# A seven-tap dynamic convolution followed by a maxout MLP: the first tokens' halo load is split into 112 and 15 partitions on two queues

## Chip, cores and metric

The kernel runs on one core of one Trainium2 chip. The metric is the device time of one execution in microseconds (us); three runs of the kernel before gave 476.36, 476.66 and 478.31, median 476.66. Profiles are of one further execution.

## What is computed

The reference takes x (8 x 4160 tokens x 192), a weight generator (8 heads x 7 taps per token) and three MLP matrices. Cut to its core:

```python
w = softmax(weight_gen, axis=-1)                      # per token and head, over K = 7 taps
x_pad = concatenate([zeros((B, 6, D)), x], axis=1)    # causal: 6 zero tokens ahead of each sequence
idx = arange(S)[:, None] + arange(7)[None, :]
a = einsum('bshk,bskhg->bshg', w, x_pad[:, idx, :])   # 8 heads of 24 channels
h1, h2 = a @ w1, a @ w2                               # 192 -> 1024
out = maximum(h1, h2) @ w_out                         # 1024 -> 192
```

A token's convolution needs the six tokens before it. Where tokens are cut into blocks, those six are the block's halo.

## The kernel before

**Tiling.** The 33,280 tokens are laid over 128 partitions, 260 consecutive tokens (CPP) each, so 16 partitions hold one sequence. They are worked in batches of 16 tokens per partition (BATCHES), and each batch in units of 8 (UNITS; 4 in batch 0). The halo of batch 0 on partition p is the last six tokens of partition p - 1: 6 x 192 floats, 4608 bytes, a row for each of partitions 1 to 127. Partition 0 has none and gets zeros (memset, L297), and each 16th partition begins a sequence, so its halo is multiplied by zero: a mask of 0 and 1 per partition (msk, L315 to L319) scales the halo on its way into xb_t (L324).

**Stages.** For a batch: ScalarE (ACT) takes exp of weight_gen (exp_sum, L109), VectorE (DVE) sums over taps (red, L114), ACT takes the log (ln, L117), DVE subtracts it (shift, L121), ACT's second exp gives normalized weights (weights, L134). DVE multiplies x by them for all seven taps (mul, L145) and adds the taps (adds, L162 to L164). The result must be transposed for TensorE (PE): in units 0 to 3 PE does it and sums the taps on the way (sum_transpose, L184, copied out by ACT, L190), later a DMA transpose (L171). The maxout is written as h1 + relu(h2 - h1): wd holds w2 - w1 (made by DVE at L375 to L380), hidden products are L209 and L220, relu is L231/L233 on ACT, and output products are L245, L254 and L259. The h1 part uses w10 = w1 @ w_out, which PE computes once from transposed w1 (L353, then L403).

**Order.** The program order on each engine is written out by hand (a manual schedule); each engine runs its instructions in that order, and waits for others by semaphores. DMAs are issued from two engines' queues: SyncE (SP) and GpSimd (POOL). Up to the loop the order that matters here is:

- SP: weight_gen of batch 0 (L87), the halo (L298), the first 4 tokens of x (xs, L303), w1 and w2 in pieces of 128 and 64 rows (ws0E, ws0T, ws1E, ws1T, L309), weight_gen of batch 1 (L87). No wait stands between them in the program.
- POOL: iota (L315), the identity matrix, then a copy (gate, L332) that reads ws0E, so that the loads behind it are issued only once ws0E has landed: x for the rest of batch 0 and for batch 1 (L97), w_out (L335), the batch halo by an SBUF copy (L103), weight_gen of batches 2 and 3. These x and w_out loads convert to bf16.
- ACT: exp_sum(0), the masked halo (L324), ln(0), the copy of xs (L327), weights(0), two copies of transposed w1 (L357), exp_sum(1), the copy of unit 0's transposed sum (L190).
- DVE: red(0), shift(0), mul(0,0), the five wd instructions, mul(0,4), red(1), mul(0,8); shift(1) after ln(1).
- PE: 50 dummy matmuls (keep_warm, L364), 24 transposes of w1 (L353), 12 dummies, sum_transpose(0), 16 dummies, then the hidden products of unit 0.

The halo's source and destination in the kernel before:

```python
nc.sync.dma_start(
    out=xs[1:P, 0:PAD * D],
    in_=bass.AP(tensor=x.tensor, offset=(CPP - PAD) * D,
                ap=[[CPP * D, P - 1], [1, PAD * D]]),
)
```

Of the kernel before, what the change touches and what calls it, by code (L numbers as in the profile page):

```python
# [23 lines left out]
def kernel(  # L24
# [9 lines left out]
    nc = tc.nc  # L34

    B, S, D = x.shape
    H, K = weight_gen.shape[2], weight_gen.shape[3]
    F = moe_w1.shape[1]
    P = 128
    PAD = K - 1  # L40
    WGC = H * K
    FCH = F // P
    CPP = B * S // P
# [246 lines left out]
    with tc.tile_pool(name="pstage", bufs=1) as pstage:  # L290
        ident_f = pstage.tile([P, P], FP32, name="ident_f")
        xs = pstage.tile([P, (PAD + 4) * D], FP32, name="xs")
        ws = {(kind, wi): pstage.tile([nr, F], FP32, name=f"ws{wi}{kind}")
              for kind, nr in (("E", P), ("T", 64)) for wi in range(2)}

        load_wg(0, nc.sync)
        nc.vector.memset(xs[0:1, 0:PAD * D], 0.0)  # L297
        nc.sync.dma_start(  # L298
            out=xs[1:P, 0:PAD * D],
            in_=bass.AP(tensor=x.tensor, offset=(CPP - PAD) * D,  # L300
                        ap=[[CPP * D, P - 1], [1, PAD * D]]),
        )
        nc.sync.dma_start(  # L303
            out=xs[:, PAD * D:],
            in_=bass.AP(tensor=x.tensor, offset=0, ap=[[CPP * D, P], [1, 4 * D]]),
        )
        for wi, wsrc in enumerate((moe_w1, moe_w2)):
            for kind, r0, nr in (("E", 0, P), ("T", P, 64)):
                nc.sync.dma_start(  # L309
                    out=ws[kind, wi],  # L310
                    in_=bass.AP(tensor=wsrc.tensor, offset=r0 * F, ap=[[F, nr], [1, F]]),
# [24 lines left out]
            out=wo[:, :].rearrange("p (f d) -> p f d", d=D),  # L336
            in_=bass.AP(tensor=moe_w_out.tensor, offset=0, ap=[[D, P], [P * D, FCH], [1, D]]),
# [198 lines left out]
```

## Time and profile before

| what | value |
|---|---|
| median of three runs | 476.66 us |
| the profiled execution | 477.96 us |
| its span, first to last instruction | 476.2 us |
| mean granted PE clock | 0.963 |
| PE busy | 435.2 us (91%) |
| DVE busy | 382.0 us (80%) |
| ACT busy | 356.6 us (75%) |
| POOL busy | 29.4 us (6%) |
| DMA bytes, mean rate | 65.84 MB, 138 GB/s |
| PE busy in the first 48 us | 20.07 us |

How to read it: the span is cut in 40 slices of 11.9 us, with one digit for each engine's busy share in tenths. PEclk is the clock that PE was granted, in tenths. The DMA row is the mean busy share of the core's 16 DMA engines, and GB/s what they moved. The chain that ended last is followed back from the last instruction, at each step to what released it; "SPq" in it is time in which SyncE's queue issues a DMA. The waits list which instruction waited for whom, in total. Landing times run from a DMA's issue to the end of its data. A busy PE is not a PE at its peak, since matmuls are pipelined and their ends are modelled.

### The profile page before, as it was taken

How to read it: one execution, taken by the hardware profiler on the slowest of the kernel's cores; microseconds unless marked ns; L12 is line 12 of the kernel's file. 1: busy time of each engine (PE TensorE's matmuls, PEld its weight loads, DVE VectorE, ACT ScalarE, POOL GpSimd, SP SyncE). 2: the span in 40 equal slices, each digit the busy share in tenths (PEclk: the TensorE clock that was granted, in tenths of full speed). 3: DMA queues.
4: the chain of work that ended last, by engine and by line, in shares of the span. 5: the costliest groups of instructions: out<-in, count | busy, mean ns of one | idle time of the engine just before them, and what ended most of it. 6: DMA issues, size and time to landing. Idle time of an engine off the chain costs nothing.

```text
span 476.2 us, 8966 instructions
## 1 busy us (share of the span) xinstructions
PE 435.2 (91%) x4014; PEld 290.9 (61%) x4014; DVE 382.0 (80%) x158; ACT 356.6 (75%) x405; POOL 29.4 (6%) x60
## 2 busy tenths in 40 slices
PE   4029998889989999999999999999999999999996
PEld 4017875456656666666666666666666666666675
DVE  2029499999999999999999999999999999990000
ACT  1033678977968888888888888889888878777762
POOL 0022101010101010101010101010100000000000
PEclk9556999999999999999999999999999999999999
DMA  1719357473778573848495847566684745333412
GB/s 56 210 37 177 81 147 141 157 162 100 188 138 207 125 206 103 213 92 204 89 209 109 198 133 161 169 143 186 123 179 111 181 105 137 100 94 92 94 73 100
DMA packets 60295, 65.84 MB, mean 138 GB/s; under 512 B 50369, under 2 KB 50881, under 8 KB 60256
## 3 DMA queue, kind: packets, MB, share of 16 engines
q1 hardware_dynamic: 53888, 41.03, 33.6%
q0 software_dynamic: 6368, 24.24, 23.2%
q8 instruction: 31, 0.51, 0.4%
q14 instruction: 8, 0.07, 0.0%
HBM read 35.96 MB, written 25.56 MB: 129 GB/s over the span
## 4 chain that ended last, share of the span: by engine, by line
PE 74%; ACT 14%; DMA 7%; SPq 3%; issue 1%; ACTq 0%
PE op_ps L259 29%; PE hdp L209 19%; PE hdp L220 13%; ACT rd_t L231 8%; PE op_ps L254 6%; DMA ws0T<-in_moe_w_dram 4%; ACT en_t L134 3%; DMA yt<-y_t 3%; PE yps L184 2%; SPq L303 2%; ACT o_t L271 2%; PE op_ps L245 2%; PE tp L353 1%; ACT rd_t L233 1%; PE warm L364 0%
## 5 line engine op out<-in xcount | busy, mean ns | idle before, releaser
L231 ACT ACTIVATE rd_t<-hdp 128x1024 bf16<-128x1024 f32 x240 | 246.5, 1029 | 63.8 <-PE hdp L209 36.7
L259 PE MATMUL op_ps<-wo,rd_t 128*128 128x192 bf16 x2080 | 214.3, 246 | 0.4 <-ACT rd_t L233 0.3
L145 DVE TENSOR_TENSOR m_t<-xb_t,en_t 128x21504 bf16<-128x21504 bf16 (+2 forms) x21 | 185.2, 8817 | 2.7 <-ACT en_t L134 2.5
L259 PEld LDWEIGHTS <-rd_t 128*128 128x128 bf16 x2080 | 175.7, 98 | 14.8 <-ACT rd_t L233 0.8
L209 PE MATMUL hdp<-yt,wdE 128*128 128x512 bf16 (+1 forms) x280 | 101.6, 364 | 4.8 <-DMA yt<-y_t 3.8
L209 PE MATMUL hdp<-yt,wdO 128*128 128x512 bf16 (+1 forms) x280 | 101.5, 364 | 0.0
L220 PE MATMUL hdp<-yt,wdR 64*128 64x512 bf16 (+1 forms) x560 | 84.6, 366 | 3.4 <-ACT rd_t L233 1.4
L162 DVE TENSOR_TENSOR m_t<-m_t 128x4608 bf16<-128x4608 bf16 (+1 forms) x31 | 78.0, 2515 | 0.5
L254 PE MATMUL op_ps<-w,yt 128*128 128x192 bf16 x260 | 65.3, 251 | 0.0
L220 PEld LDWEIGHTS <-wdR 64*128 64x128 bf16 x560 | 20.9, 94 | 66.7 <-issue 65.4
L254 PEld LDWEIGHTS <-yt 128*128 128x128 bf16 x260 | 25.1, 97 | 50.3 <-issue 36.0
L163 DVE TENSOR_TENSOR m_t<-m_t 128x3072 bf16<-128x3072 bf16 (+1 forms) x31 | 53.7, 1732 | 1.1
L271 ACT COPY o_t<-op_ps 128x768 f32<-128x768 f32 x65 | 51.9, 799 | 2.6 <-issue 2.6
L121 DVE TENSOR_TENSOR wg_t<-wg_t,sum_t 128x896 f32<-128x896 f32 (+1 forms) x17 | 17.7, 1043 | 31.1 <-ACT sum_t L117 31.1
L134 ACT ACTIVATE en_t<-wg_t 128x1024 bf16<-128x1024 f32 (+5 forms) x36 | 33.4, 937 | 0.4 <-DVE wg_t L121 0.4
L245 PE MATMUL op_ps<-w,yt 64*128 64x192 bf16 x260 | 32.5, 242 | 0.2 <-ACT w L409 0.2
L209 PEld LDWEIGHTS <-wdE 128*128 128x128 bf16 x280 | 27.4, 98 | 7.6 <-DMA yt<-y_t 4.3
L97 POOL DMA_DIRECT2D xb_t<-in_x_dram x20 | 10.9, 548 | 323.2 <-DVE m_t L145 323.2
L164 DVE TENSOR_TENSOR y_t<-m_t 128x1536 bf16<-128x1536 bf16 (+1 forms) x31 | 29.3, 945 | 1.1
L353 PE MATMUL tp<-ident_f,ws0E 128*128 128x128 f32 (+1 forms) x16 | 5.8, 390 | 25.0 <-DMA ws0E<-in_moe_w_dram 25.0
L209 PEld LDWEIGHTS <-wdO 128*128 128x128 bf16 x280 | 27.4, 98 | 1.9 <-issue 1.7
L233 ACT ACTIVATE rd_t<-hdp 128x1024 bf16<-128x1024 f32 x20 | 20.4, 1025 | 10.1 <-PE hdp L209 10.1
(40 smaller groups left out, 135.4 us busy)
## 6 DMA issues: line engine op xcount, KB each, us to landing
out_dram<-o_t SPq DMA_DIRECT2D x30, 768.0 KB, 3.7
xb_t<-in_x_dram POOLq DMA_DIRECT2D x14, 768.0 KB, 7.0
wg_t<-in_weight_gen_dram POOLq DMA_DIRECT2D x14, 448.0 KB, 7.8
xb_t<-xb_t POOLq DMA_DIRECT2D x16, 288.0 KB, 7.2
out_dram<-o_t SPq DMA_DIRECT2D x5, 384.0 KB, 2.3
wg_t<-in_weight_gen_dram SPq DMA_DIRECT2D x2, 448.0 KB, 9.9
xb_t<-in_x_dram POOLq DMA_DIRECT2D x4, 192.0 KB, 4.1
xb_t<-in_x_dram POOLq DMA_DIRECT2D x2, 384.0 KB, 7.2
```

The lines of the kernel that those rows point to most:

```text
L134: nc.scalar.activation(out=_sub(en_ts[b, o], k0 * N * 2, [[2 * N, k1 - k0], [2, N], [1, 2]]), in_=_sub(wg_ts[b], o * WGC + k0, [[1, k1 - k ...
L145: nc.vector.tensor_tensor(out=m_ts[b][:, K * o * D:K * (o + n) * D], in0=_sub(xb_ts[b], o * D, [[D, K], [1, n * D]]), in1=_sub(en_ts.pop(( ...
L162: nc.vector.tensor_tensor(out=taps(0, 1, 3), in0=taps(0, 1, 3), in1=taps(3, 1, 3), op=ALU.add)
L163: nc.vector.tensor_tensor(out=taps(0, 2, 2), in0=taps(0, 2, 2), in1=taps(1, 5, 2), op=ALU.add)
L164: nc.vector.tensor_tensor(out=y_ts[b][:, (o + a) * D:(o + a + w) * D], in0=taps(0, 1, 1), in1=taps(2, 1, 1), op=ALU.add)
L209: nc.tensor.matmul(hid_out(u, f, j), lhsT=wd[kind][:, f * P:(f + 1) * P], rhs=_sub(yt_ts[u], 2 * j * P, [[3 * P, n // 2], [1, P]]), start= ...
L220: nc.tensor.matmul(hid_out(u, f, j), lhsT=wd["R"][r, f * P:(f + 1) * P], rhs=_sub(yt_ts[u][r, :], P, [[3 * P, n // 2], [1, P]]), start=fir ...
L231: nc.scalar.activation(out=rd_ts[u][:, f, :], in_=hd_ts.pop((u, f)), func=AF.Relu)
L245: nc.tensor.matmul(op_ts[u, i // 2][:, at:at + D], lhsT=yt_ts[u][r, (3 * i + 1) * P:(3 * i + 2) * P], rhs=w10[r, 2 * D:3 * D], start=(i % ...
L254: nc.tensor.matmul(op[:, at:at + D], lhsT=yt[:, (3 * i + 2 * j) * P:(3 * i + 2 * j + 1) * P], rhs=w10[:, j * D:(j + 1) * D], start=False, ...
L259: nc.tensor.matmul(op[:, at:at + D], lhsT=rd[:, f, j * 512 + i * P:j * 512 + (i + 1) * P], rhs=wo[:, f * D:(f + 1) * D], start=False, stop ...
L271: nc.scalar.copy(out=_sub(o_ts[u], 4 * g * D, [[2 * D, 2], [D, 2], [1, D]]), in_=_sub(op_ts.pop((u, g)), 0, [[D, 2], [512, 2], [1, D]]))
```

## The change

The load of 127 halo rows from the SP queue becomes two: partitions 16 to 127 (112 rows) from the SP queue, in the same place, and partitions 1 to 15 (15 rows) from the POOL queue. Bytes, source, destination and all other instructions are the same. The new POOL DMA comes first in POOL's program, ahead of the iota and the identity. The reader of the halo, ACT's scaled copy, now waits for both. All later line numbers move up by one.

```diff
         nc.vector.memset(xs[0:1, 0:PAD * D], 0.0)
-        nc.sync.dma_start(
-            out=xs[1:P, 0:PAD * D],
-            in_=bass.AP(tensor=x.tensor, offset=(CPP - PAD) * D,
-                        ap=[[CPP * D, P - 1], [1, PAD * D]]),
-        )
+        for p0, p1, eng in ((16, P, nc.sync), (1, 16, nc.gpsimd)):
+            eng.dma_start(
+                out=xs[p0:p1, 0:PAD * D],
+                in_=bass.AP(tensor=x.tensor, offset=(p0 * CPP - PAD) * D,
+                            ap=[[CPP * D, p1 - p0], [1, PAD * D]]),
+            )
         nc.sync.dma_start(
             out=xs[:, PAD * D:],
             in_=bass.AP(tensor=x.tensor, offset=0, ap=[[CPP * D, P], [1, 4 * D]]),
```

## The prediction

> **What bounds the kernel now.** I read the page first: its slices, then the chain that ended last.
>
> ```profile
> span 476.2 us, 8966 instructions
> ...
> PE   4029998889989999999999999999999999999996
> ...
> PEclk9556999999999999999999999999999999999999
> DMA  1719357473778573848495847566684745333412
> ...
> PE 74%; ACT 14%; DMA 7%; SPq 3%; issue 1%; ACTq 0%
> ```
>
> One slice is 11.9 us. From the fourth slice on TensorE (PE) is busy nine tenths or more almost throughout, and the chain is mostly PE. The first three slices are different: PE is idle, its clock falls to half, and the chain's DMA and SPq shares sit there. So next the chain's own pieces, in order of time (start us, length us, what):
>
> ```profile
> 1.20 0.32 SPq L298
> ...
> 1.58 10.87 SPq L303
> ...
> 12.49 1.35 SPq L309
> ...
> 13.88 19.35 DMA ws0T<-in_moe_w_dram
> ...
> 33.27 6.12 PE tp L353 x23
> 39.39 1.40 PE warm L364 x12
> 40.79 4.25 PE yps L184 x42
> ```
>
> The end is set by an unbroken PE chain that begins at 33.27, when the second w1 piece (ws0T) has landed. Before it the SP queue stands in the issue of L303 for 10.87 us, right behind the halo (L298), and ws0T then takes 19.35 us for 256 KB. The waits say who feels it (total us, times, longest):
>
> ```profile
> POOL gate L332 <- DMA ws0E<-in_moe_w_dram: 31.2, 1, 31.2
> ...
> ACT xb_t L324 <- DMA xs<-in_x_dram: 25.5, 1, 25.5
> ...
> PE tp L353 <- DMA ws0E<-in_moe_w_dram: 25.0, 1, 25.0
> ```
>
> Last, stretches of the head. Columns after the length: busy us and (count) of PE, PEld, DVE, ACT and POOL, then granted clock, DMA share, GB/s.
>
> ```profile
> 8.00:12.00 4.00, 0.00 (x0) 0.00 (x0) 0.00 (x0) 0.00 (x0) 0.00 (x0) 0.82 0.06 26
> 12.00:20.00 8.00, 0.00 (x0) 0.00 (x0) 0.00 (x0) 0.00 (x0) 0.00 (x0) 0.50 0.75 213
> ...
> 28.00:32.00 4.00, 0.00 (x0) 0.00 (x0) 0.04 (x1) 1.52 (x3) 0.00 (x0) 0.50 0.06 26
> ```
>
> A share of 0.06 is 1/16: of 16 DMA engines one works, at 26 GB/s, both before and after the other loads pass (12 to 24 us).
>
> **What that engine carries.** The halo is 127 x 4608 B = 0.585 MB; a sixteenth of the SP loads after it (0.393 xs + 1.573 weights + 0.459 second weight_gen = 2.425 MB) is 0.152 MB. Together 0.737 MB, at 26 GB/s 28.3 us, from 3.7 us (first weight_gen in) to 32.0. The weight loads were complete at 32.6 to 33.2. So I read it thus: the whole halo goes through one engine, and each later load has a sixteenth queued there and is complete only after it. The other fifteen engines were done at 24.
>
> **Part 1: the 127-partition load becomes 112 (SP) + 15 (GpSimd).** [...]
>
> *New arrival times.* SP issues at 0.74 and then every 0.42 us (0.32 to 0.40 plus gaps in its rows): all eight by 4.1 us, ahead of the data; I assume no queue fills, since no engine has more than a sixteenth of anything. For the rate:
>
> ```profile
> DMA packets 728, 2.46 MB, mean 234 GB/s; under 512 B 88, under 2 KB 88, under 8 KB 728
> ```
>
> That is 13.0 to 23.5 us, these same loads on the fifteen free engines: 234 GB/s. The best in the trace is the first weight_gen load, 358 and 346 GB/s in its two full half-microseconds. I take 234, being the same loads. First weight_gen data end at 3.6 as now. Both halo parts and xs: 0.978 MB, 4.2 us, to 7.8. Add 0.5 (the first weight_gen data ended near 3.5, its Exp began at 4.04): ACT L324 starts at 8.3, now 30.48. ws0E and ws0T: 0.786 MB, 3.4 us, to 11.1, with the 0.5 **11.6**, now 33.27. PE's chain starts **21.7 us earlier**. At 350 GB/s it would start at 9.1 (24.2 saved), at 200 at 12.9 (20.4).
>
> *Does the rest follow?* What comes before PE's needs, now and shifted by 21.7: DVE needs 6.2 us from the start of L324 to the end of the first product (36.69 - 30.48): 14.5; PE wants it for L184 at 40.79 - 21.7 = 19.1. The wd matrices need ws1E and ws1T: 0.786 MB more, 15 us alone; then 3.8 us of DVE work (36.60 to 40.41), 18.8; PE wants them at 45.93 - 21.7 = 24.2. Both are covered by about 5 us. From 58 us to 125 DVE is without a gap and PE waits for it (yt, 5.0 and 8.2 us in the chain at 102 and 126), but DVE's last waits before that are for ACT results that follow PE, so DVE shifts with PE and gives nothing back.
>
> **Part 2: the new GpSimd DMA.** It stands in POOL's order before the iota and the identity. A POOL load row is 548 ns each (the w_out one 914): ident, now at 2.38, comes 0.55 to 0.9 late, PE's first 50 keep-warm matmuls (2.65 to 7.73) too; PE then idles till the weights come, so on the path 0. SP's x load and the weights are not behind it. ACT L324 now waits for it as well, and behind L324 in ACT's order stand the Ln, the copy of xs and the weights, so DVE. POOL loads of 192 KB, nearly three times its 68 KB, landed in 4.1 us (median), the slowest near them in 7.4: 15 rows issued at 0.84 are there by 5 to 9, and cover lasts until PE wants the first product: 19.1 - 6.2 = 12.9. Cost 0; each us later than 12.9 would cost one. Below nothing it can't go, beyond what part 1 counts.
>
> **Part 3: what the earlier gate triggers.** POOL's later loads wait on ws0E (gate, L332), now landing near 10.6 in place of 32.65. Today they have the engines to themselves:
>
> ```profile
> q0 software_dynamic: 1607, 1.36, 100.1%
> ```
>
> That row is 34.0 to 43.5 us: POOL's queue fills all 16 engines for 9.5 us. After the change, 1.1 MB of SP's loads (most of ws1E, ws1T, second weight_gen) are still under way when they start near 12. Alone those need 4.8 us; sharing half and half about 9.6, so the second weight_gen is in near 22, and POOL's loads end near 26. ACT's exp_sum(1) waits for the former and stands *before* the yt copy that PE needs; that copy is due at 45.08 - 21.7 = 23.4, so the Exp (0.95) must start by 22.4. Cover: 0.4 us, so between 0 (SP served first) and 4 us (POOL first: 26). I take **+0.7**. ws1T by 20, wd by 22, still under 24.2. POOL's own loads are wanted later: w_out at 30.4 (52.14 now), x for mul(1,0) at 36.6 (58.35 now), with L103 by 32: covered.
>
> **Part 4: the clock.** PE's matmuls ran 102 ns each in the first 50 and 106 in L184 at 40.8, but 60 in L184 at 49: the head works at half clock. The granted clock fell at 10.7, 3.0 us after the first block ended, stayed 0.50 through all 6 us of transposes and rose at 44.6, 5.3 us after dense matmuls began. [...] With the warm block ending near 8.3 the fall comes near 11.3, so at most the first transposes run fast. Between 0 and -4 (transposes and L184 at half their time, the rest then waiting for wd and exp_sum(1)); I take **-0.5**.
>
> **Sum.** -21.7 + 0.7 - 0.5 = -21.5 us. The profiled run took 477.96 (span 476.2 and 1.76 around it), so it would give 456.5. The runs' median is 476.66, 1.30 below the profiled one; from it: **455.2 us**, 4.5% faster.
>
> **The rivals.**
> - *Better than that* (0.11): loads near 350 GB/s, or the clock still up when the weights come: -24 to -28, 449 to 452.5. For: the first load's rate, and a shorter idle gap. Against: 234 for these very loads, and 0.50 through the transposes.
> - *The collision of part 3 bites* (0.12): the second weight_gen, or ws1T, lands 4 to 8 us later than PE wants it: 459 to 463. For: 0.4 us of cover. Against: 5 us of cover everywhere else.
> - *The split does not spread* (0.03): 112 partitions stay on one engine, 0.069 MB leaves it: 2.7 us, 474. Against: 64 partitions spread.
> - *Slower* (0.02): the GpSimd part lands late and holds ACT at L324, and with it DVE's whole head. By part 2 each us past 12.9 costs one, so the gain is gone when it lands at 34.4 and the kernel is 0.5% slower past 37; at 40, 479. Nearest rows say 4 to 7 us of flight, so it would have to take five times that.
>
> **How the numbers follow.** The likeliest case (0.72) is 452.5 to 459. Leaving out some of the first two rivals' ends, 450 to 461 holds about 8 in 10 and a little over. 0.5% (2.4 us) is about what can be told from no change here. Faster 0.95, within 0.03 (half of the third rival, and a chance of something unseen), slower 0.02.
>
> **What would show it.** Right: no stretch at a 0.06 share; SP's issues all under 1 us and done by 5; L324 near 8.3; tp near 11.6; yt copy at 23 to 24; L209 to the end as long as now (45.93 to 476). Wrong: SP still standing in an issue, tp after 13.5, ACT waiting at exp_sum(1) for more than 1 us, or a new DMA wait of DVE after 20 us. The prediction fails if the shift at the first tp does not arrive whole at the last matmul.

## The result and the profile after

| | before | after |
|---|---|---|
| median | 476.99 us (4 runs) | 454.19 us (4 runs) |
| profiled execution | 477.96 us | 453.83 us |
| its span | 476.2 us | 452.1 us |
| ACT's masked halo starts | 30.48 us | 7.06 us |
| first w1 transpose that needs ws0T | 33.27 us | 10.54 us |
| first hidden product (L209) | 45.93 us | 22.27 us |
| from there to the end of the span | 430.27 us | 429.83 us |

The ratio after to before is 0.9521 (95% interval 0.9495 to 0.9548): 4.8% faster. 455.2 was predicted, with a range of 450 to 461.

The page of the changed kernel, the rows that were shown of before:

```profile
span 452.1 us, 8967 instructions
...
PE   4999989899999999999999999999999999999996
...
PEclk9699999899999999999999999999999999999999
DMA  8936475637784839483957657393948363334312
...
PE 80%; ACT 15%; DMA 3%; issue 1%; SPq 0%; ACTq 0%
```

The hole in PE's second and third slice is gone, the DMA engines are busy from the first slice on, and the chain's DMA share has gone from 7% to 3%, its SPq share from 3% to 0%. The chain's head, in order of time (start, length, what):

```profile
1.20 0.41 SPq L299
1.67 0.42 SPq L304
2.12 0.43 SPq L310
2.60 7.90 DMA ws0T<-in_moe_w_dram
10.54 6.12 PE tp L354 x23
16.67 1.40 PE warm L365 x12
18.06 3.32 PE yps L184 x42
21.38 0.89 PE warm L365 x16
```

SP no longer stands in the issue of xs (0.42 us, 10.87 before), and ws0T takes 7.90 us in place of 19.35. The transposes last 6.12 us as before; PE's first sum takes 3.32 in place of 4.25, a matter of the clock (below). The waits of the first 60 us:

```profile
POOL gate L333 <- DMA ws0E<-in_moe_w_dram: 6.8, 1, 6.8
...
PE tp L354 <- DMA ws0E<-in_moe_w_dram: 2.1, 1, 2.1
ACT xb_t L325 <- DMA xs<-in_x_dram: 1.6, 1, 1.6
```

31.2, 25.0 and 25.5 us have become 6.8, 2.1 and 1.6. One stretch of the head in both kernels, 4 to 10 us, first after and then before (the last two columns are DMA share and GB/s):

```profile
4.00:10.00 6.00, 3.87 (x44) 3.51 (x41) 2.18 (x2) 3.46 (x5) 0.48 (x2) 0.98 1.03 291
```

```profile
4.00:10.00 6.00, 3.72 (x40) 3.55 (x37) 1.09 (x1) 0.95 (x1) 0.00 (x0) 1.00 0.06 25
```

All 16 engines at 291 GB/s where one moved 25. (The share of 1.03 is past 1, so records of packets overlap here; a share of about 1 is read as all sixteen busy.)

### The profile page after: what moved, and what is told of

Its sections match the earlier page's. It is cut to its first block, busy times and chain, and to the rows that moved or that the text cites. A ratio compares the mean times of both kernels' runs of the same rounds, so it can differ in the third digit from the quotient of the medians.

```text
span 452.1 us, 8967 instructions
## 1 busy us (share of the span) xinstructions
PE 435.1 (96%) x4014; PEld 290.5 (64%) x4014; DVE 382.3 (85%) x158; ACT 356.5 (79%) x405; POOL 29.7 (7%) x61
## 4 chain that ended last, share of the span: by engine, by line
PE 80%; ACT 15%; DMA 3%; issue 1%; SPq 0%; ACTq 0%
PE op_ps L259 32%; PE hdp L209 21%; PE hdp L220 14%; ACT rd_t L231 8%; PE op_ps L254 7%; ACT en_t L134 3%; ACT o_t L271 2%; PE yps L184 2%; PE op_ps L245 2%; DMA ws0T<-in_moe_w_dram 2%; PE tp L354 1%; DMA yt<-y_t 1%; ACT rd_t L233 1%; PE warm L365 1%; PE pw L404 0%
## 5 line engine op out<-in xcount | busy, mean ns | idle before, releaser
L209 PE MATMUL hdp<-yt,wdE 128*128 128x512 bf16 (+1 forms) x280 | 102.0, 365 | 2.9 <-DMA yt<-y_t 1.9
L209 PE MATMUL hdp<-yt,wdO 128*128 128x512 bf16 (+1 forms) x280 | 101.8, 365 | 0.0
L209 PEld LDWEIGHTS <-wdE 128*128 128x128 bf16 x280 | 27.5, 98 | 5.5 <-issue 3.0
L209 PEld LDWEIGHTS <-wdO 128*128 128x128 bf16 x280 | 27.5, 98 | 1.9 <-issue 1.7
L233 ACT ACTIVATE rd_t<-hdp 128x1024 bf16<-128x1024 f32 x20 | 20.4, 1024 | 10.2 <-PE hdp L209 10.1
L114 DVE TENSOR_REDUCE sum_t<-e_t 128x128 f32<-128x896 f32 (+1 forms) x17 | 17.7, 1041 | 9.2 <-ACT e_t L109 9.1
```

Source lines behind the costliest of these rows:

```text
L209: nc.tensor.matmul(hid_out(u, f, j), lhsT=wd[kind][:, f * P:(f + 1) * P], rhs=_sub(yt_ts[u], 2 * j * P, [[3 * P, n // 2], [1, P]]), start= ...
```

## Experiments

The theory: the halo's *number of partitions* decides over how many DMA engines SP's load is spread; with 127 it was one (0.06 of sixteen, 25 GB/s), and what stood behind it waited (ws0T took 19.35 us). The rivals: two queues, or a smaller transfer, make the gain. In all kernels here what is computed is unchanged. The last column is the span from the first hidden product on.

| kernel | ws0T's first transpose | first hidden product | span | rest |
|---|---|---|---|---|
| before | 33.27 | 45.93 | 476.2 | 430.27 |
| after | 10.54 | 22.27 | 452.1 | 429.83 |
| 113 + 14 | 30.76 | 42.09 | 472.0 | 429.91 |
| 112 + 15, both SP | 10.46 | 21.21 | 452.2 | 430.99 |
| 122 + 5 | 23.89 | 35.21 | 465.6 | 430.39 |
| 127 from GpSimd | 11.09 | 21.74 | 451.8 | 430.06 |
| 127 from ACT | 19.04 | 52.92 | 483.4 | 430.48 |
| 15 rows late | 10.88 | 26.41 | 456.5 | 430.09 |
| xs cut too | 10.68 | 22.86 | 453.7 | 430.84 |
| w1 first | 8.38 | 22.11 | 452.4 | 430.29 |
| after, again | 10.92 | 21.73 | 451.6 | 429.87 |
| w1 first, 36 dummies | 8.61 | 21.02 | 452.1 | 431.08 |
| 85 dummies first | 10.63 | 21.64 | 452.9 | 431.26 |

From the first hidden product on, every kernel takes 430.5 us within 0.8, while the start of that product differs by up to 32 us. All but about 1.4 us of the differences between these kernels is made before it.

**113 and 14 partitions.** One row moved; still two DMAs on two queues.

```diff
-        for p0, p1, eng in ((16, P, nc.sync), (1, 16, nc.gpsimd)):
+        for p0, p1, eng in ((15, P, nc.sync), (1, 15, nc.gpsimd)):
```

> The split is moved by one row: 113 partitions from SP and 14 from GpSimd, still two DMAs on two queues. Theory (the number of partitions decides over how many DMA engines a load is spread, and 113 is a prime, so one engine): 0.521 MB on one engine, 0.064 MB less than before, 2.5 us at 26 GB/s, so about 474.5 us, a DMA share of 0.06 in the head, first w1 transpose with ws0T near 31. Rival (two queues or a smaller transfer make the gain): 454, as with 112.

Measured: 475.3 us, ratio to before 0.9949 (0.9926 to 0.9972). The stretch of 24 to 28 us:

```profile
24.00:28.00 4.00, 0.00 (x0) 0.00 (x0) 0.00 (x0) 0.02 (x1) 0.00 (x0) 0.50 0.06 26
```

And in its chain SP stands in the issue of xs again:

```profile
1.55 8.44 SPq L304
```

The one busy engine is back, and nearly the whole gain is gone for one row. The fourteen rows taken off it (0.0645 MB) bring 33.27 - 30.76 = 2.51 us, which is 25.7 GB/s, one engine's pace. Two queues or a smaller transfer do not make the gain.

**Both parts from SP.**

```diff
-        for p0, p1, eng in ((16, P, nc.sync), (1, 16, nc.gpsimd)):
+        for p0, p1, eng in ((16, P, nc.sync), (1, 16, nc.sync)):
```

> 112 and 15 partitions as in the change, but both DMAs from SP's queue, the 15 right behind the 112. Theory (spreading is all): 15 partitions go to 15 engines, one more SP issue (0.4 us) ahead of the weights, and the identity is 0.4 us earlier on GpSimd: 454 to 455, within 0.3% of the change. Rival (the second queue matters): most of the gain goes, 465 or more.

Measured: 454.68 us, ratio 0.9531 (0.9503 to 0.9559), the change's 0.9521 within it. The second queue is not what gains.

This run also settles a rival that the other two cuts of SP's load leave open. All of SP's parts end at partition 127, so with the count their first partition changes as well: 16 in the change, 15 with 113 partitions, 6 with 122 (next). The spread could come from a first partition that is a multiple of 16. But here SP's queue also carries the 15 rows that begin at partition 1 (KB, us from issue to landing):

```profile
xs<-in_x_dram SPq DMA_DIRECT2D x1, 504.0 KB, 4.8
xs<-in_x_dram SPq DMA_DIRECT2D x1, 67.5 KB, 4.9
```

They land as fast as the 112. In the trace all 127 packets of 4608 B lie between 3.3 and 5.5 us; at their mean of 0.22 us, the fifteen one after another would take 3.3 us alone. So these rows were spread too (over how many engines is not shown), and among these loads it is the count that goes with the spread, not the first partition.

**122 and 5 partitions.**

```diff
-        for p0, p1, eng in ((16, P, nc.sync), (1, 16, nc.gpsimd)):
+        for p0, p1, eng in ((6, P, nc.sync), (1, 6, nc.gpsimd)):
```

> 122 partitions from SP and 5 from GpSimd. Theory: 122 is 2 x 61, so two engines with 0.281 MB each and their sixteenths of the rest (0.152 MB): 0.433 MB at 26 GB/s is 16.7 us, done near 20 in place of 32; the first transpose with ws0T near 20, 463 to 464 us, DMA share near 0.12 in the gaps. Rival (queues): 454.

Measured: 467.8 us, ratio 0.9806 (0.9791 to 0.9821). 16 to 20 us:

```profile
16.00:20.00 4.00, 0.00 (x0) 0.00 (x0) 0.00 (x0) 0.00 (x0) 0.00 (x0) 0.50 0.13 51
```

Share 0.13 is 2/16 and 51 GB/s is twice the rate of one: two engines, as expected for 122. The time is about 4 us over what I expected, because I gave the two engines 26 GB/s from the start. While all sixteen were busy they moved less each: 247 GB/s together from 3.6 to 8 us and 197 from 8 to 12, so 15 and then 12. If shared evenly, that is 0.12 of the 0.433 MB of each of the two; the other 0.31 at 26 GB/s end near 24 (an estimate), and the transpose came at 23.89.

**127 partitions from GpSimd, not split.**

```diff
-        for p0, p1, eng in ((16, P, nc.sync), (1, 16, nc.gpsimd)):
+        for p0, p1, eng in ((1, P, nc.gpsimd),):
```

> The halo undivided, 127 partitions in one DMA, but from GpSimd's queue. If one engine for 127 holds on that queue too: SP's loads share that engine with it and are no longer behind it, w1 is in near 12, but ACT's masked halo waits until near 30, so DVE's first product is late: 468 to 474. If GpSimd's queue spreads 127 rows: 454 to 455, and the split itself is not needed.

Measured: 454.19 us, ratio 0.9524 (0.9503 to 0.9545). 2 to 10 us:

```profile
DMA packets 677, 2.32 MB, mean 290 GB/s; under 512 B 80, under 2 KB 80, under 8 KB 677
...
q0 software_dynamic: 144, 0.59, 26.5%
```

q0 is GpSimd's queue: it carried the whole 0.59 MB of halo inside these 8 us. On one engine, at 26 GB/s, that takes over 20. GpSimd's queue spread these 127 rows (0.59 MB in 8 us is 74 GB/s, nearly three times one engine's 26), SP's did not; the split itself isn't needed.

**127 partitions from ACT's queue.**

```diff
-        for p0, p1, eng in ((16, P, nc.sync), (1, 16, nc.gpsimd)):
+        for p0, p1, eng in ((1, P, nc.scalar),):
```

> The halo undivided, 127 partitions in one DMA, from ACT's queue. Theory (the load sits on one DMA engine, whichever of SP's and ACT's queues issues it, and the queue behind it is a second, separate cost): SP's issues run through by 5 us, w1 is in by 11 to 14, but the halo needs the one engine until about 30 and ACT's masked halo, DVE's first product and PE's first sum wait for it: 472 to 476, although the weights came 20 us earlier. If only the standing queue cost time: 454 to 457.

Measured: 485.71 us, slower than before: ratio 1.0182 (1.0157 to 1.0206). The chain's head, then the queues from 26 to 40 us (packets, MB, share of 16 engines):

```profile
0.77 41.02 DMA xs<-in_x_dram
...
41.87 1.25 ACT xb_t L325
```

```profile
q0 software_dynamic: 163, 0.27, 10.6%
q10 hardware_dynamic: 59, 0.27, 5.0%
q1 hardware_dynamic: 4, 0.01, 0.2%
```

The place of the wait is as expected (the first product waits for the halo), the size is not: the halo is in at 41.8, not 30. SP's loads (q1) and, once the gate opens at 18, GpSimd's (q0) also have a part on the halo's engine, ahead of or among the packets of ACT's queue (q10): in the trace, between 34 and 36.5 us, every halo packet follows one of GpSimd's, and no other packet runs. In the kernel before, GpSimd's loads stayed behind the gate until the halo was through. Halo, SP's sixteenth with the first weight_gen, and GpSimd's sixteenth (1.36 MB / 16) are 0.585 + 0.181 + 0.085 = 0.85 MB; at the 22 to 26 GB/s that this one engine moved between 28 and 40 us, that is 33 to 39 us, from about 1.5. I had left GpSimd's part out; the rest of the gap to 41.8 I did not take apart. SP's queue was free by 4.6 us and w1 still came only at 19: a free queue didn't help here, where one engine had the halo and a sixteenth of every load.

**The GpSimd part late.** Its DMA is moved behind the gate copy, which is itself written ahead of ACT's first instructions so that the reader follows.

```diff
-        for p0, p1, eng in ((16, P, nc.sync), (1, 16, nc.gpsimd)):
+        for p0, p1, eng in ((16, P, nc.sync),):
...
+        nc.gpsimd.tensor_copy(out=gate, in_=ws["E", 0][:, 0:1])
+        for p0, p1, eng in ((1, 16, nc.gpsimd),):
+            eng.dma_start(
+                out=xs[p0:p1, 0:PAD * D],
+                in_=bass.AP(tensor=x.tensor, offset=(p0 * CPP - PAD) * D,
+                            ap=[[CPP * D, p1 - p0], [1, PAD * D]]),
+            )
         exp_sum(0)
...
-        nc.gpsimd.tensor_copy(out=gate, in_=ws["E", 0][:, 0:1])
```

> The change, but GpSimd's 15 rows are issued behind the gate, so near 9.5 us, landing near 15. The prediction's cover: PE wants the first product 6.2 us after the masked halo starts, in the changed kernel at 18.06, so the halo may come by 11.9 for nothing, and each us past that costs one: about 3.5 us, 457 to 459. If the halo's time has no bearing: 454.

Measured: 458.94 us, ratio 0.9629 (0.96 to 0.9658). The chain:

```profile
9.65 5.61 DMA xs<-in_x_dram
15.34 1.25 ACT xb_t L332
...
18.59 2.97 DVE m_t L145
21.60 3.92 PE yps L184 x42
```

From the halo's reader to PE's first sum are 6.26 us, and the sum starts 3.54 later than in the change. The wait for the halo is covered until about 12 us, and past that it moves the sum one for one. The span is 4.4 us longer than the change's: these 3.54, 0.60 because the sum itself takes 3.92 us in place of 3.32, and 0.26 behind it.

**xs cut in two as well.**

```diff
-        nc.sync.dma_start(
-            out=xs[:, PAD * D:],
-            in_=bass.AP(tensor=x.tensor, offset=0, ap=[[CPP * D, P], [1, 4 * D]]),
-        )
+        for p0, p1, eng in ((64, P, nc.sync), (0, 64, nc.gpsimd)):
+            eng.dma_start(
+                out=xs[p0:p1, PAD * D:],
+                in_=bass.AP(tensor=x.tensor, offset=p0 * CPP * D, ap=[[CPP * D, p1 - p0], [1, 4 * D]]),
+            )
```

> The change, and the xs load (128 partitions, already spread) is also cut in two, 64 partitions from SP and 64 from GpSimd. Theory (a cut pays only where it changes the spread): no difference from the change, 453.5 to 455.5. Rival (two queues load faster): the first transpose a microsecond or more earlier than 10.54, 453 or less.

Measured: 455.19 us, ratio 0.9545 (0.951 to 0.9581); ws0T's transpose at 10.68 against 10.54. Cutting this load, which was spread already, gained nothing.

**w1 ahead of the halo.** In SP's order: weight_gen, ws0E, ws0T, halo, xs, ws1E, ws1T. The loop over the two matrices' pieces becomes a function, load_w, called once for each matrix.

```diff
         load_wg(0, nc.sync)
+        load_w(0, moe_w1)
...
-        for wi, wsrc in enumerate((moe_w1, moe_w2)):
...
+        load_w(1, moe_w2)
```

> The change, with both w1 pieces ahead of the halo and xs in SP's queue. The head is now bound by bytes: at 297 GB/s the 0.786 MB of w1 are in near 6.7 in place of 10.54, the halo and xs near 10; then DVE's first product (10 + 6.2 = 16.2) and no longer w1 sets PE's first sum, now 18.06: 1.5 to 3 us less than the change, 451 to 453. If the head's end were set by anything else: 454.

Measured: 454.39 us, ratio 0.9524 (0.9503 to 0.9544): nothing gained. The chain:

```profile
2.27 7.71 DMA xs<-in_x_dram
...
13.34 2.97 DVE m_t L145
16.36 4.66 PE yps L184 x42
21.02 1.26 PE warm L368 x16
```

PE's first sum does start 1.70 us earlier, near where I had it (16.2), but it then takes 4.66 us in place of 3.32, and the dummies 1.26 in place of 0.89. The transposes had ended by 12.9; behind them came the 12 dummies, and then PE was idle for 2.1 us until DVE's product. The clock:

```profile
18.00:20.00 2.00, 2.00 (x22) 2.00 (x20) 1.94 (x3) 0.00 (x0) 0.00 (x0) 0.50 1.23 223
```

was still at 0.50 at 20 us. Of the 1.70 us, 1.34 were lost in the sum at half clock, and the first hidden product came only 0.16 earlier than in the change.

**w1 first, with the wait filled; and a longer warm-up of the change.** To test that, and with the change again beside them. The three expectations below are, in this order, for the change once more, for w1 first with 36 dummies in place of 12, and for the change with 85 first dummies in place of 50.

```diff
-        keep_warm(12)
+        keep_warm(36)
```

```diff
-        keep_warm(50)
+        keep_warm(85)
```

> The changed kernel as it is, beside the next two on the same chip: 454 to 455.

> As with w1 ahead of the halo, and the 12 dummy matmuls between the transposes and the first sum are 36, to fill the wait for the first product (14.0 to 16.3) and to have the clock up in it. Clock theory (w1 first gave nothing because PE's first sum then ran wholly at half clock, 4.45 us in place of 3.32): the sum takes 2.4 to 3.4 us, the first hidden product starts near 20.2, bound by the wd matrices (done at 20.0) and no longer by PE; 430.3 more is 450.5 of span, 451.5 to 453 as a run. If the clock isn't it: as w1 first, 454.4.

> The change, with 85 first dummy matmuls in place of 50, so that PE is busy until the weights come (9.5). If the clock's fall by idling is what slows the transposes: they run at full clock until about 3 us after the dummies, take 4.6 to 5.5 us in place of 6.1, and the first hidden product starts 0.7 to 1.5 us earlier: 452.7 to 453.5. If transposes run at that pace anyway: 454.2.

Measured: 453.22, 453.64 and 453.43 us; ratios 0.9509 (0.9494 to 0.9525), 0.9508 (0.9482 to 0.9534) and 0.951 (0.949 to 0.953). No difference in time. With w1 first and 36 dummies the clock did come up earlier (0.88 on average from 18 to 20 us, 0.50 with 12 dummies) and the sum took 3.11 us in place of 4.66; the first hidden product started at 21.02, 0.71 before that of the change beside it, not at the 20.2 that I expected. So it was the clock that had slowed the sum. Yet its rest is 1.21 longer. The chains of the two, the one with 36 dummies first:

```profile
77.06 6.50 DMA yt<-y_t
```

```profile
77.79 5.12 DMA yt<-y_t
```

The transposing DMA that PE waits for was released 0.73 earlier and took 1.38 longer. The 85 dummies show the same DMA at 6.49. With them the transposes took 4.71 us, within what I expected, but the first hidden product came only 0.09 earlier (21.64 against 21.73), not 0.7 to 1.5: the clock fell to 0.50 in the transposes, near 13.3, and was up again only at about 20, so the sum took 4.01 us in place of 3.38. The change's own second profile had its clock up until past 12 us as it was (transposes 5.15 us), so that run tests the warm-up poorly. No version was found that beats the change; why that DMA took 5.1 us in one and 6.5 in another stays open.

## Why the prediction was right, and by how much its terms were off

The mechanism was right: one engine for 127 partitions (0.06 of sixteen at 25 GB/s, 4 to 10 us), sixteen for 112 (1.03 at 291), and the shift at the first transpose, 22.73 us, arrived whole at the end. No miss hid another: each of the four terms came out lower than was put down for it. The sum was -21.5 us of span; measured were 452.1 - 476.2 = -24.1. In terms:

| term | predicted | measured |
|---|---|---|
| start of PE's chain (ws0T in) | -21.7 | -22.73 |
| collision with GpSimd's loads | +0.7 | 0 |
| clock before the first hidden product | -0.5 | -0.93 |
| from there to the end | 0 | -0.44 |
| sum | -21.5 | -24.10 |

- *Start.* That 112 rows go over all sixteen engines, no row of before shows; this term took it for granted, and the 1.03 of sixteen at 291 GB/s showed it only afterwards. It also assumed that SP's queue would not fill, and none of SP's eight issues stood: they took 0.40 to 0.61 us each. I took 234 GB/s from the same loads in the trace of before. There fifteen engines carried them and SP was kept standing in its issues; with sixteen and SP's issues done by 5.0 us it was 291. The prediction's own sum with 291 gives 10.2; measured were 10.54. The first load's 350 would have been too high. What held the rate at 234 before is not shown in full: fifteen sixteenths of 291 are 273, and from 20.5 to 23.5 us, with SP's issues over, it was 241.
- *Collision.* ACT's second Exp started at 17.61, straight behind the w1 copy, and waited for nothing: the second weight_gen, issued at 4.38, landed 9.7 later at 14.1, not at 22. SP's queue moved its last 1.04 MB after 10 us in 4.1 us, 250 GB/s, although GpSimd's first load was issued at 9.64. So two things in this term were wrong: at 12 us 0.39 MB of SP's were left, not 1.1, and from 12 to 14 us these went beside only 0.14 MB of GpSimd's, not half and half.
- *GpSimd's DMA.* It cost nothing, as said: issue 0.66 us, identity 0.35 later, landed at 7.0, covered until 12 (shown by the run with the 15 rows late).
- *Clock.* The transposes ran at 0.50 as predicted (6.12 us both times). The gain came in PE's first sum instead: the clock rose 3.4 us after dense matmuls began (16.6 to 20.0), 5.3 before. With 113 partitions, where PE had stood idle for 21.7 us, the same sum took 2.93. In the change's second profile the clock fell only at 12.7, in place of 9.7, and part of the transposes ran fast (5.15 us). So this term is a spread of about a microsecond between executions rather than a gain of the change. The first 50 dummies in before took 102 ns each at a granted clock of 1.00 (2.6 to 6.6 us), so their pace, unlike that of L184 at 40.8 (0.50), shows no half clock.
- *The rest.* A second wait for a transposing DMA (8.23 us in the chain at 125.86) is not in the chain of after; it is again in that of 112 + 15 from SP, at 101.14 (8.97 us). The profile of after has another loss, which that of before has not: behind its wait at 78.32 the clock is at half for about 3 us (row below), and there two groups of output products take 1.15 and 1.28 us, against 0.66 in the profile before. So the -0.44 is what is left of pieces of either sign; I do not count it as the change's doing.

```profile
85.00:88.00 3.00, 3.00 (x18) 2.35 (x16) 3.00 (x2) 2.19 (x3) 0.00 (x0) 0.50 0.35 145
```

- *Two transfers in place of one* gained nothing where the load was spread already (xs cut, 455.19 us against 454.19); where it was on one engine they gained 22.8 us.

That the terms miss by 2.6 us and the median by 1.0 comes from the reference points: the profiled execution of before was 1.0 us above the median of its runs, that of after 0.4 below, and the median of before, 476.66 with three runs, is 476.99 with four.

## What to carry to other kernels

Look at the DMA share before the GB/s: 0.06 of sixteen engines, at 25 or 26 GB/s, was one engine here, and the loads with a piece queued on it were complete only behind the halo (ws0T took 19.35 us, and 7.90 in the change). From SP's queue the loads of 15, 64, 112 and 128 partitions were spread, those of 113 and 127 were on one engine and that of 122 on two. So where a share shows one engine, another count is worth a run, with the remainder as a DMA of its own. Here the remainder from SP (454.68 us) or from GpSimd (454.19) and all 127 rows from GpSimd (454.19) came to the same; all 127 from ACT's queue was worse than before (485.71). With the head bound by bytes (1.03 of sixteen engines), a microsecond won in it had still to pass the clock and the next DMA wait: of the 1.70 us of w1 first 0.16 were left at the first hidden product, and of the 0.71 with 36 dummies nothing at the end.

## What the runs showed of the hardware

- One row made the difference: 112 partitions from SP 454.2 us, 113 partitions 475.3.
- The same 127 rows, issued at about 1 us: their reader starts at 30.48 from SP's queue, at 9.21 from GpSimd's, at 41.87 from ACT's.
- One engine moved 26 GB/s alone (before, 8 to 12 us). At a share of about 1 it was 18 each in the change (291 GB/s from 4 to 10 us, divided by 16), 15 and 12 with 122 partitions (247 from 3.6 to 8, 197 from 8 to 12).
- Float transposes on PE, 6 us of them, neither raised the clock (0.50 from 10 to 20 us in the profile after, and 0.50 through them before) nor held it (it fell near 11.4 in the run with w1 first, in the midst of them, which lasted from 8.2 to 12.9).
